# Moving half of one output projection earlier, adding its strips off TensorE, and running the other projection in half-width strips, in a two-attention decode kernel

## The chip, the cores and the metric

The kernel runs on one core of a Trainium2 chip. The time is the device time of one execution in microseconds (us). A second number, the *span*, runs from the first to the last instruction in the trace of the program. Times inside a trace are counted from the start of the span.

TensorE is the matmul engine, VectorE and ScalarE the two engines that read its results from PSUM. In profile lines they are PE (PEld for its weight loads), DVE and ACT; SPq is the queue that issues the DMAs.

## The reference

Two attention layers decode one token each; the two results are joined.

```python
# A: 32 heads, each with its own K and V of 32768 x 128
q = (x @ wq).reshape(B, Sq, H, Dh).transpose(0, 2, 1, 3)
p = softmax(einsum("bhqd,bhkd->bhqk", q, k_cache) * Dh ** -0.5)
o = einsum("bhqk,bhkd->bhqd", p, v_cache)
a = o.transpose(0, 2, 1, 3).reshape(B, Sq, H * Dh) @ wo      # (4096,) @ (4096, 512)
# B: the same with 8 shared K/V heads and the last 4096 keys only
out = concatenate([a, b], axis=-1)
```

All data is bf16. Some 570 MB have to be read, nearly all of it K and V of A.

## The kernel before

A short first stage does all of B's attention. A loop over A's 32 heads follows: transposes of K on TensorE, copies of these by VectorE, scores, softmax, and PV (probabilities times V). VectorE reduces PV's four strips into `oc`, and a *gather* matmul adds the head's row to a collecting PSUM bank. Last come the two output projections with `wo`, each as 32 matmuls of one output row ("row" a below) accumulated in PSUM. Wo is loaded at the end of the load queue, behind the last K and V.

```python
        for g in range(NQH):
            self.loop = {"pe": g, "dve": g // 2}
            self.load_k(g, 1 if 0 < g < NQH - 1 else 2)
            self.load_v(g)
            self.emit_qcopy(g)
            self.emit_unit("A", g)          # transposes of K and scores
            self.emit_stats("A", g)         # softmax
            self.emit_PT("A", g)
            self.emit_PV("A", g)            # PV, reduction by VectorE, gather
        self.loop = {}
        for n in ("B", "A"):
            for part in range(len(self.WO_CUTS[n]) - 1):
                self.load_wo(n, part)
        self.emit_spread("A")               # divide by the sums, turn o for the projection
        self.emit_proj()

    WO_CUTS = {"A": (0, 11, 19, 25, 29, 31, 32), "B": (0, 16, 32)}   # the parts in which Wo is loaded

    def halves(self, e, bank, lhsT, rhs, begin, end, only=(0, 1)):   # one row as two strips of 256
        for i in only:
            inst = e.matmul(bank[64 * i:64 * i + 1, 0:256], lhsT=lhsT, rhs=rhs[:, 256 * i:256 * i + 256], start=begin,
                            stop=end, tile_position=(0, 64 * i), skip_group_check=True)
        return inst

    def emit_proj(self):
        top = self.WO_CUTS["A"][1]
        for part in range(len(self.WO_CUTS["B"]) - 1):       # B: rows go to four strips, 32 partitions apart
            o = self.proj_part("B", part, lambda e, lhsT, rhs, a: e.matmul(
                self.S[32 * (a % 4):32 * (a % 4) + 1, :], ...))
        strips = self.op("dve", lambda v: v.tensor_copy(self.pb[:, :], self.S[:, :]), o)
        rows = o = self.op("pe", lambda e: e.matmul(self.ACC[0:1, :], lhsT=self.e32[:, 0:1], rhs=self.pb[:, :], ...))
        o = self.op("dve", lambda v: v.tensor_copy(self.qrow[0:1, :], self.ACC[0:1, :]), o)
        # ... B's half of the output leaves ...
        row = self.proj_part("A", 0, ...)                     # A, part 0: rows 0 to 10 at full width
        row = self.op("dve", lambda v: v.tensor_copy(self.pb[0:1, :], self.T[1][0:1, :]), row, rows)
        for part in range(1, len(self.WO_CUTS["A"]) - 1):     # A, the other parts: two half-width strips
            if part == 3:                                     # add the row of part 0
                self.op("pe", lambda e: self.halves(e, self.PT, self.e32[0:1, 0:1], self.pb[0:1, :], False, False), row)
            self.proj_part("A", part, ...)
        # ... row 31, stores of the two halves by VectorE and ScalarE, output DMA ...
```

## Time and profile before

| what | before |
|---|---|
| time, 3 runs | 1323.59 us (1322.69 to 1323.95) |
| span of the profiled run | 1321.7 us |
| bytes loaded, mean rate | 570.6 MB at 432 GB/s |
| last landing of a load (Wo of A, last part) | 1318.82 |
| start of the final stores | 1320.05 |

Three lines of the profile page of the kernel before: busy time of the engines (share of the span), the DMA's packets and rate, and the share of the 16 DMA engines' time that the load queue took.

```profile
PE 968.2 (73%) x13243; PEld 673.7 (51%) x13243; DVE 750.7 (57%) x1341; ACT 55.1 (4%) x168; POOL 2.6 (0%) x22
DMA packets 13359, 570.59 MB, mean 432 GB/s; under 512 B 1570, under 2 KB 1700, under 8 KB 2084
q1 hardware_dynamic: 13060, 570.43, 99.8%
```

The load queue is never out of work. The Trainium skill ("DMA: Bandwidth & Descriptors", Specifications) puts the fabric's ceiling at 435 GB/s, and the trace's 432 agrees. So the body of the kernel is a wall of bytes. What can still move is what comes after the last landing.

The chain of waits of the kernel before, its last 20 us. Columns: start, length, what ran (engine, output, line, count).

```profile
1300.21 6.30 PE psACC L656 x49
1306.52 0.08 PE psG L683 x2
...
1308.19 0.42 PE psG L683 x2
...
1309.67 3.27 PE psS L733 x32
...
1312.97 0.70 DVE pb L736
...
1313.71 1.02 PE psACC L737 x2
1314.73 2.27 PE psT L741 x11
1317.01 3.02 PE psPT L719 x42
...
1320.05 0.41 DVE out_sb L726
```

No load is in this chain: PV (L656), the gather (L683), B's projection (L733), the copy and row sum of B's strips (L736, L737), A's first part (L741) and its other parts (L719) follow one another on TensorE, and the last store starts at 1320.05, which is 1.23 us after the last landing.

The windows view of the kernel before near the end. Columns: stretch, its length, busy us of PE, PEld, DVE, ACT and POOL with instruction counts, the granted TensorE clock (1.00 is full), the DMA share, GB/s.

```profile
1309.00:1310.00 1.00, 0.60 (x12) 0.29 (x16) 0.35 (x2) 0.00 (x0) 0.00 (x0) 0.55 0.92 394
...
1311.00:1312.00 1.00, 1.00 (x16) 0.28 (x8) 0.00 (x0) 0.00 (x0) 0.00 (x0) 0.50 0.96 408
1312.00:1313.00 1.00, 0.91 (x12) 0.14 (x4) 0.03 (x1) 0.00 (x0) 0.00 (x0) 0.75 0.99 420
...
1318.00:1319.00 1.00, 1.00 (x13) 0.35 (x10) 0.00 (x0) 0.00 (x0) 0.00 (x0) 1.00 0.17 57
1319.00:1320.00 1.00, 1.00 (x16) 0.52 (x14) 0.00 (x0) 0.00 (x0) 0.00 (x0) 1.00 0.00 0
```

The DMA has stopped by 1319 while TensorE works for another microsecond. And B's projection ran at half clock: the third number from the end is 0.50.

### The profile page before, as it was taken

The numbers are of one execution on the slowest core, as the hardware profiler recorded it, in microseconds if no ns is written. First come the engines' busy times: TensorE is split into PE (matmuls) and PEld (weight loads), VectorE is DVE, ScalarE is ACT, GpSimd is POOL, SyncE is SP. The second block draws the span as 40 slices with busy tenths as digits, with TensorE's granted clock in tenths as the row PEclk, the third lists the DMA queues.
The fourth block names the chain that finished last, engine by engine and source line by source line (L and its number), as shares of the span: only waits on it lengthen the run. The fifth ranks groups of instructions, "written<-read, shape, count | busy, mean of one in ns | idle before, by whom it ended". The sixth has DMA issues, their size and how long they took to land. (4 is left out here: it accounts for less than half of the span.)

```text
span 1321.7 us, 28783 instructions
## 1 busy us (share of the span) xinstructions
PE 968.2 (73%) x13243; PEld 673.7 (51%) x13243; DVE 750.7 (57%) x1341; ACT 55.1 (4%) x168; POOL 2.6 (0%) x22
## 2 busy tenths in 40 slices
PE   4675768777677878767787777678777667877787
PEld 3353446555444655544465544446554445555453
DVE  3563556664555666455566645556665456665563
ACT  0000000000000000000000000000000000000000
POOL 0000000000000000000000000000000000000000
PEclk9886788887878888787888878888887788888788
DMA  9999999999999999999999999999999999999998
GB/s 404 434 434 431 440 434 434 434 436 432 433 436 436 428 438 434 428 438 434 428 442 430 428 442 432 430 438 434 437 432 432 438 430 434 438 428 436 436 428 365
DMA packets 13359, 570.59 MB, mean 432 GB/s; under 512 B 1570, under 2 KB 1700, under 8 KB 2084
## 3 DMA queue, kind: packets, MB, share of 16 engines
q1 hardware_dynamic: 13060, 570.43, 99.8%
q8 instruction: 8, 0.13, 0.0%
q10 hardware_dynamic: 288, 0.00, 0.0%
q14 instruction: 3, 0.02, 0.0%
HBM read 570.43 MB, written 0.00 MB: 432 GB/s over the span
## 5 line engine op out<-in xcount | busy, mean ns | idle before, releaser
L557 DVE COPY kt<-psT 128x1024 bf16<-128x1024 bf16 x1056 | 654.3, 683 | 236.9 <-PE psT L553 235.5
L553 PE MATMUL psT<-ident,kbuf 128*128 128x128 bf16 x8448 | 577.8, 234 | 169.0 <-DMA kbuf<-in_A_k_cache_dram 154.4
L553 PEld LDWEIGHTS psT<-ident,kbuf 128*128 128x128 bf16 x8448 | 538.1, 106 | 261.2 <-DMA kbuf<-in_A_k_cache_dram 162.5
L656 PE MATMUL psACC<-vbuf,ptsb 128*4 128x512 bf16 (+1 forms) x2112 | 187.0, 531 | 22.8 <-ACT ptsb L631 22.0
L576 PE MATMUL psS<-kt,qw 128*32 128x512 bf16 x2048 | 157.7, 385 | 14.9 <-DVE kt L557 14.9
L670 DVE TENSOR_SCALAR oc_A<-psACC,hot_A 128x128 f32<-128x128 f32 x32 | 11.2, 350 | 251.9 <-PE psG L683 251.9
L656 PEld LDWEIGHTS psACC<-vbuf,ptsb 128*4 128x4 bf16 (+1 forms) x2112 | 59.8, 111 | 140.4 <-issue 93.1
L604 ACT ACTIVATE psb<-psS,nb_A 128x512 bf16<-128x512 f32 x32 | 22.0, 687 | 1166.5 <-DVE nb_A L603 1166.5
L576 PEld LDWEIGHTS psS<-kt,qw 128*32 128x32 bf16 x2048 | 34.0, 95 | 57.6 <-DVE kt L557 30.8
L683 PE MATMUL psG<-oc_A,hw 128*32 128x128 f32 (+1 forms) x128 | 19.3, 227 | 52.3 <-DVE oc_A L672 52.3
L683 PEld LDWEIGHTS psG<-oc_A,hw 128*32 128x32 f32 x128 | 11.4, 109 | 62.4 <-DVE oc_A L672 55.0
L628 PE MATMUL psPT<-ident,psb 128*128 128x128 bf16 x136 | 18.3, 279 | 34.0 <-ACT psb L604 34.0
L672 DVE SCALAR_TENSOR_TENSOR oc_A<-psACC,hot_A,oc_A 128x128 f32<-128x128 f32 x96 | 33.6, 350 | 3.4
L593 DVE TENSOR_REDUCE tr_in<-psS 128x1 f32<-128x512 f32 x34 | 23.5, 692 | 17.2 <-PE psS L576 17.2
L628 PEld LDWEIGHTS psPT<-ident,psb 128*128 128x128 bf16 x136 | 10.3, 119 | 37.1 <-ACT psb L604 36.7
L597 PE MATMUL psACC<-rows,tr_in 128*1 128x64 f32 x64 | 8.7, 217 | 25.6 <-DVE tr_in L593 25.6
L631 ACT ACTIVATE ptsb<-psPT 128x512 bf16<-128x512 bf16 x34 | 20.3, 597 | 30.9 <-PE psPT L628 30.9
L597 PEld LDWEIGHTS psACC<-rows,tr_in 128*1 128x1 f32 x64 | 2.7, 81 | 35.1 <-DVE tr_in L593 35.1
L601 PE MATMUL psACC<-mr_A,nscale 1*128 1x1 f32 x64 | 12.1, 256 | 9.8 <-DVE mr_A L600 9.8
L601 PEld LDWEIGHTS psACC<-mr_A,nscale 1*128 1x128 f32 x64 | 9.4, 182 | 15.8 <-DVE mr_A L600 15.8
L603 DVE COPY nb_A<-psACC 128x1 f32<-128x1 f32 x32 | 5.0, 157 | 15.1 <-PE psACC L601 15.1
L600 DVE TENSOR_REDUCE mr_A<-psACC 1x1 f32<-1x64 f32 x32 | 6.8, 213 | 11.7 <-PE psACC L597 11.7
(82 smaller groups left out, 74.9 us busy)
## 6 DMA issues: line engine op xcount, KB each, us to landing
kbuf<-in_A_k_cache_dram SPq DMA_DIRECT2D x4, 4096.0 KB, 23.2
kbuf<-in_B_k_cache_dram SPq DMA_DIRECT2D x2, 4096.0 KB, 31.6
vbuf<-in_B_v_cache_dram SPq DMA_DIRECT2D x2, 4096.0 KB, 25.4
vbuf<-in_B_wq_dram SPq DMA_DIRECT2D x1, 4096.0 KB, 12.4
vbuf<-in_A_wq_dram SPq DMA_DIRECT2D x1, 4096.0 KB, 31.9
kbuf<-in_B_wo_dram SPq DMA_DIRECT2D x2, 2048.0 KB, 33.1
kbuf<-in_A_wo_dram SPq DMA_DIRECT2D x1, 1408.0 KB, 27.4
kbuf<-in_A_wo_dram SPq DMA_DIRECT2D x1, 1024.0 KB, 29.5
```

The source lines that it names most:

```text
L553: inst = e.transpose(T[:, 128 * k:128 * k + 128], src[:, DH * k:DH * k + DH], self.ident[:, :])
L557: self.copies.append(self.op("dve", lambda v: v.tensor_copy(KT[:, :], T[:, :]), o, to="pe"))
L576: inst = e.matmul(self.S[32 * c:32 * c + 32, :], lhsT=win, rhs=self.kt[(bb + c // 2) % NKT][:, 512 * (c % 2):512 * (c % 2) + 512], start=b ...
L593: o = dve(lambda v: v.reduce_max(tr["in"][:, 0:1], self.S[:, :], axis=AXX), self.sdone, self.k_pool, to="pe" if name == "A" else None)
L597: o = self.op("pe", lambda e: e.matmul(self.ACC[0:1, 0:64], lhsT=tr["in"][:, 0:1], rhs=self.rows64[:, :], start=True, stop=True, skip_grou ...
L601: o = self.op("pe", lambda e: e.matmul(self.ACC[:, 64:65], lhsT=self.nscale[:, :], rhs=t["mr"][0:1, :], start=True, stop=True, skip_group_ ...
L604: self.sread = self.op("act", lambda s: s.activation(out=self.psb[:, :], in_=self.S[:, :], func=ACTF.Exp, bias=t["nb"][:, k:k + 1], scale= ...
L628: inst = e.transpose(PT[:, 128 * jj:128 * jj + 128], self.psb[:, 128 * jj:128 * jj + 128], self.ident[:, :])
L631: self.ptread = self.op("act", lambda s: s.activation(out=self.ptsb[:, :], in_=PT[:, 0:512], func=ACTF.Copy), self.psread, to="pe")
L656: inst = e.matmul(acc[32 * c:32 * c + rows, 0:512], lhsT=lhsT, rhs=rhs, start=begin, stop=end, tile_position=(0, 32 * c), skip_group_check ...
L672: o = self.op("dve", lambda v, src=src, hot=hot: v.scalar_tensor_tensor(out=oc, in0=src, scalar=hot, in1=oc, op0=ALU.mult, op1=ALU.add), p ...
L683: return self.op("pe", lambda e: e.matmul(self.G[0:32, c0 + c:c0 + c2], lhsT=win, rhs=t["oc"][g % len(t["oc"])][:, c:c2], start=False, sto ...
```

## The change

The intent is to shorten TensorE's last stretch in four ways:

1. The gather of head g moves from the end of pass g to the top of pass g + 1, so the last one can be placed freely behind the loop.
2. Half of B's projection runs before that last gather, in TensorE's wait for VectorE.
3. B's four strips are added by VectorE and ScalarE instead of by a copy and an fp32 matmul.
4. All of A's rows run as two half-width strips, so there is no full-width row to be added to them.

```diff
             self.emit_qcopy(g)
+            self.gath = self.emit_gather("A", g - 1, 0, DH)
             self.emit_unit("A", g)
@@
+        self.emit_proj_b(0)
+        self.gath = self.emit_gather("A", NQH - 1, 0, DH)
         self.emit_spread("A")
         self.emit_proj()
@@
         self.accread = o
-        self.gath = self.emit_gather(name, g, 0, DH)
+        if name == "B":
+            self.gath = self.emit_gather(name, g, 0, DH)
@@ (cut: the new helper emit_proj_b, one part of B's projection as before)
+    def sum_strips(self, o):
+        S = [self.S[32 * c:32 * c + 1, :] for c in range(STRIPS)]
+        row = [self.kt[c][0:1, :].bitcast(F32) for c in range(STRIPS)]
@@ (cut: helpers)
+        two = self.op("dve", lambda v: v.tensor_copy(row[2], S[2]), o, to="act")
+        one, three = act(1), act(3)
+        x = add(row[0], S[0], row[1], o, one)
+        y = add(row[2], row[2], row[3], two, three)
+        return add(self.qrow[0:1, :], row[0], row[2], x, y)
@@
-        strips = self.op("dve", lambda v: v.tensor_copy(self.pb[:, :], self.S[:, :]), o)
-        rows = o = self.op("pe", lambda e: e.matmul(self.ACC[0:1, :], lhsT=self.e32[:, 0:1], ...
-        o = self.op("dve", lambda v: v.tensor_copy(self.qrow[0:1, :], self.ACC[0:1, :]), o)
+        o = self.emit_proj_b(1)
+        o = self.sum_strips(o)
@@
-        row = self.proj_part("A", 0, ...)
-        row = self.op("dve", lambda v: v.tensor_copy(self.pb[0:1, :], self.T[1][0:1, :]), row, rows)
-        for part in range(1, len(self.WO_CUTS["A"]) - 1):
-            if part == 3:
-                self.op("pe", lambda e: self.halves(e, self.PT, self.e32[0:1, 0:1], self.pb[0:1, :], False, False), row)
-            self.proj_part("A", part, lambda e, lhsT, rhs, a: self.halves(e, self.PT, lhsT, rhs, a == top, False)
+        for part in range(len(self.WO_CUTS["A"]) - 1):
+            self.proj_part("A", part, lambda e, lhsT, rhs, a: self.halves(e, self.PT, lhsT, rhs, a == 0, False)
                            if a < 31 else None)
```

The first gather of the loop has no head before it; `oc` and its selection `hw` are set to zero for it, which is cut here.

More of the change, by code (lines that the diff above doesn't have):

```diff
@@ L284, in alloc @@
         self.m4 = sb("m4", [1, 128], F32)
-        self.pb = sb("pb", [128, 512], F32)
         self.out_sb = sb("out_sb", [1, 512], BF16)
@@ L456, in constants @@
             pattern=[[-32, 4], [-1, 16]], compare_op=ALU.is_equal, fill=0.0, base=0, channel_multiplier=1), rows)
+        pool(lambda g: g.memset(c["A"]["oc"][0][:, :], 0.0))
+        self.k_hw = pool(lambda g: g.memset(self.hw[:, :], 0.0))
         pool(lambda g: g.memset(self.nscale[:, :], -self.SCALE))
@@ L460, in constants @@
             self.k_pool = pool(lambda g, n=n: g.memset(c[n]["b"][:, :], 0.0))
-        self.k_hw = pool(lambda g: g.memset(self.hw[:, :], 0.0))
         dve = lambda fn, *deps, **k: self.op("dve", fn, *deps, **k)
@@ L684, in emit_gather @@
             self.G[0:32, c0 + c:c0 + c2], lhsT=win, rhs=t["oc"][g % len(t["oc"])][:, c:c2], start=False, stop=True,
-            skip_group_check=True), self.accread, self.sread, self.hcopy if name == "A" else self.k_sel, to="dve")
+            skip_group_check=True), *(self.accread, self.sread, self.hcopy if name == "A" else self.k_sel) if g >= 0 else
+            (self.k_hw, self.accread), to="dve")
     def emit_spread(self, name):
@@ L727, in store @@
         return self.op("act", lambda e: e.activation(out=out, in_=src, func=ACTF.Copy), dep)
-    def emit_proj(self):
-        top = self.WO_CUTS["A"][1]
-        for part in range(len(self.WO_CUTS["B"]) - 1):
-            o = self.proj_part("B", part, lambda e, lhsT, rhs, a: e.matmul(
-                self.S[32 * (a % 4):32 * (a % 4) + 1, :], lhsT=lhsT, rhs=rhs, start=(a < 4), stop=(a >= 28),
-                tile_position=(0, 32 * (a % 4)), skip_group_check=True))
-        strips = self.op("dve", lambda v: v.tensor_copy(self.pb[:, :], self.S[:, :]), o)
-        rows = o = self.op("pe", lambda e: e.matmul(self.ACC[0:1, :], lhsT=self.e32[:, 0:1], rhs=self.pb[:, :], start=True,
-                                             stop=True, skip_group_check=True), strips, self.accread)
-        o = self.op("dve", lambda v: v.tensor_copy(self.qrow[0:1, :], self.ACC[0:1, :]), o)
-        self.op("sp", lambda e: e.dma_start(self.out[0, :, 512:1024], self.qrow[0:1, :]).then_inc(self.outsem["B"], 16), o)
-        row = self.proj_part("A", 0, lambda e, lhsT, rhs, a: e.matmul(
-            self.T[1][0:1, :], lhsT=lhsT, rhs=rhs, start=(a == 0), stop=(a == top - 1), skip_group_check=True))
-        row = self.op("dve", lambda v: v.tensor_copy(self.pb[0:1, :], self.T[1][0:1, :]), row, rows)
-        for part in range(1, len(self.WO_CUTS["A"]) - 1):
-            if part == 3:
-                self.op("pe", lambda e: self.halves(e, self.PT, self.e32[0:1, 0:1], self.pb[0:1, :], False, False), row)
-            self.proj_part("A", part, lambda e, lhsT, rhs, a: self.halves(e, self.PT, lhsT, rhs, a == top, False)
@@ new lines, in emit_proj_b @@
+    def emit_proj_b(self, part):
+        return self.proj_part("B", part, lambda e, lhsT, rhs, a: e.matmul(
+            self.S[32 * (a % 4):32 * (a % 4) + 1, :], lhsT=lhsT, rhs=rhs, start=(a < 4), stop=(a >= 28),
+            tile_position=(0, 32 * (a % 4)), skip_group_check=True))
+    def sum_strips(self, o):
+        S = [self.S[32 * c:32 * c + 1, :] for c in range(STRIPS)]
+        row = [self.kt[c][0:1, :].bitcast(F32) for c in range(STRIPS)]
+        dve = lambda fn, *deps: self.op("dve", fn, *deps)
+        act = lambda c: self.op("act", lambda e: e.activation(out=row[c], in_=S[c], func=ACTF.Copy), two)
+        add = lambda out, a, b, *deps: dve(lambda v: v.tensor_tensor(out=out, in0=a, in1=b, op=ALU.add), *deps)
+        two = self.op("dve", lambda v: v.tensor_copy(row[2], S[2]), o, to="act")
[3 more added lines that the diff above has]
+        return add(self.qrow[0:1, :], row[0], row[2], x, y)
```

## The prediction

> **What bounds the kernel.** The page's DMA line: 570.6 MB at a mean of 432 GB/s, the load queue taking 99.8% of 16 engines' span. The Trainium skill ("DMA: Bandwidth & Descriptors", Specifications) gives a fabric ceiling of 435 GB/s; this trace agrees, so all but the last microseconds is a wall of bytes that the change does not touch. TensorE (73% busy) and VectorE (57%) have slack. Only what comes after the last landings can move.
>
> **The tail.** From the DMA issue times plus times to landing (us from the span's start): V of the last head lands at 1299.2; Wo of B in two parts at 1304.2 and 1308.9; the six parts of A's Wo at 1312.2, 1314.8, 1316.7, 1317.9, 1318.4 and 1318.9. In the windows view the DMA share falls to half at 1317 and to zero at about 1318.4. The chain of waits ends: B's projection 3.27 us, VectorE copy 0.70, fp32 row sum 1.02, A's first part at full width 2.27, the rest in halves 3.02 with the fp32 addition of the row in it (0.52), stores from 1320.05, output DMA issued 1320.55, end 1321.7. So TensorE ends about 1.1 us after the last weights landed: that backlog is the prize.
>
> **What the change does.**
> - Half of B's projection (16 of 32 matmuls, about 1.65 us) moves into the 1.64 us in which TensorE waits for VectorE's last reduction (idle before the final gather). Its weights landed at 1304.2, so nothing waits.
> - The copy and fp32 row sum leave TensorE's way: 0.76 + 1.02 us. In their place VectorE and ScalarE do six one-row operations of 0.4 to 0.7 us, hidden under A's projection.
> - A's first 11 rows cost 0.133 us a pair of halves (14 halves took 0.93 us) instead of 0.206 at full width: 0.8 us less; the row's copy and fp32 addition go (0.52 us).
> - The gather of the previous head goes to the top of the next pass. VectorE's reduction then overlaps the loop's branch: about 1 us of TensorE per pass. In the loop it buys nothing, the DMA bounds; in the last pass PV can start just when V lands, up to 0.9 us earlier.
>
> TensorE work of some 4 to 5 us leaves the tail, but A's parts then wait for their weights. Estimate: B's second half from 1308.9 to 1310.6; A's parts each 1.46, 1.06, 0.80, 0.53 and 0.27 us after their landings, so each ends before or about when the next lands. The last pair starts at 1318.95, 0.27 us to the first half, stores from about 1319.25 instead of 1320.05. Gain 0.8 us of 1323.6, or 0.06%, inside the run-to-run spread of 1.3.
>
> **Prediction:** 1322.8 us, 8 in 10 between 1321.9 and 1323.7. Faster by over 2%: 0.003; within 2%: 0.994; slower: 0.003.
>
> **What the profile would show.** Right: mean GB/s and the loop's groups unchanged; B's first half directly before the final gather; TensorE idle before several of A's parts, released by the DMA of A's weights; stores starting within 0.4 us of the last landing. The clock (granted 0.5 from about 1309.5 to 1312.5 now) may fall elsewhere. By the Trainium skill ("TensorE: Matmul & The Clock Gate", Part 1) idle windows halve it; a cold final stretch would double the last parts' matmul time and eat 0.2 to 0.5 us.
>
> **What would make it wrong.** The last landing moving by itself; a cold clock for A's parts; the early half of B's projection delaying the gather.

## The result, and the profile after

| | before | after |
|---|---|---|
| time, 6 runs each | 1322.76 us (1322.49 to 1323.95) | 1322.66 us (1321.93 to 1323.56) |
| ratio, 95% interval | | 0.9998 (0.9985 to 1.0011) |
| span of the profiled run | 1321.7 us | 1320.6 us |
| last landing | 1318.82 | 1318.63 |
| start of the final stores | 1320.05 | 1318.98 |
| stores behind the last landing | 1.23 us | 0.35 us |

A ratio here is the mean time of one kernel's fast runs over that of the other's of the same rounds, so it is not quite the ratio of the medians quoted. The kernel before is at 1323.59 us in the first table and at 1322.76 here because three more runs have been added.

The same three lines of the page of the kernel after:

```profile
PE 966.4 (73%) x13250; PEld 676.3 (51%) x13250; DVE 752.3 (57%) x1342; ACT 56.3 (4%) x170; POOL 2.8 (0%) x23
DMA packets 13359, 570.59 MB, mean 432 GB/s; under 512 B 1570, under 2 KB 1700, under 8 KB 2084
q1 hardware_dynamic: 13060, 570.43, 99.9%
```

The wall is as it was. The chain of waits of the kernel after, its last 37 us:

```profile
1283.20 28.90 DMA kbuf<-in_A_wo_dram
1312.10 0.04 issue
1312.15 4.31 PE psPT L724 x38
1316.46 0.03 issue
1316.49 2.46 PE psPT L724 x25
...
1318.98 0.41 DVE out_sb L731
```

Now a load stands at the head of the chain: A's projection (L724) starts when the first part of Wo lands and goes on as the others land. The timeline of the kernel after shows what became of TensorE's time (columns: start, length, engine, line, operation, shapes, count; in brackets the idle time before it and what ended it):

```profile
1299.16 5.92 PE L659 MATMUL psACC<-vbuf,ptsb 128*4 128x512 bf16 x64 [1.26 <-DMA vbuf<-in_A_v_cache_dram]
...
1304.97 1.02 PE L736 MATMUL psS<-kbuf,oz_B 128*1 128x512 bf16 x13
...
1306.75 0.41 PE L687 MATMUL psG<-oc_A,hw 128*32 128x128 f32 x2 [0.75 <-DVE oc_A L675]
...
1308.82 1.03 PE L736 MATMUL psS<-kbuf,oz_B 128*1 128x512 bf16 x16 [0.78 <-DMA kbuf<-in_B_wo_dram]
...
1312.15 6.80 PE L724 MATMUL psPT<-kbuf,oz_A 128*1 128x256 bf16 x64 [2.29 <-DMA kbuf<-in_A_wo_dram]
```

PV starts with V's landing (1299.02). B's first half (L736, 1304.97) sits before the last gather (L687). TensorE waits for loads three times: 1.26 us for V, 0.78 us for B's second part and 2.29 us for A's first. What left TensorE came back as waits.

The windows view of the kernel after:

```profile
1316.00:1317.00 1.00, 0.97 (x12) 0.35 (x8) 0.00 (x0) 0.00 (x0) 0.00 (x0) 0.50 1.01 398
1317.00:1318.00 1.00, 1.00 (x16) 0.49 (x14) 0.00 (x0) 0.00 (x0) 0.00 (x0) 0.75 0.62 235
1318.00:1319.00 1.00, 0.95 (x14) 0.21 (x8) 0.02 (x1) 0.00 (x0) 0.00 (x0) 1.00 0.11 36
```

The half-clock stretch has moved into A's projection, and it cost nothing that shows, since that projection waits for its weights and the last rows ran at full clock again.

One trace of each says: 1.07 us gained at the stores (1320.05 to 1318.98). Six runs of each say: 0.1 us in the median, far inside the interval. The experiments ask what the profiled gain is made of, and why the repeated runs show less of it.

### The profile page after: what moved, and what is told of

Read it like the earlier page. It is cut to its first block, busy times and chain, and to the rows that moved or that the text cites. A ratio compares the mean times of both kernels' runs of the same rounds, so it can differ in the third digit from the quotient of the medians.

```text
span 1320.6 us, 28803 instructions
## 1 busy us (share of the span) xinstructions
PE 966.4 (73%) x13250; PEld 676.3 (51%) x13250; DVE 752.3 (57%) x1342; ACT 56.3 (4%) x170; POOL 2.8 (0%) x23
## 2 busy tenths in 40 slices
DMA packets 13359, 570.59 MB, mean 432 GB/s; under 512 B 1570, under 2 KB 1700, under 8 KB 2084
## 4 chain that ended last, share of the span: by engine, by line
DMA 70%; PE 28%; DVE 1%; issue 0%; ACT 0%; SPq 0%
DMA kbuf<-in_A_k_cache_dram 65%; PE psT L556 24%; PE psS L579 4%; DMA kbuf<-in_B_k_cache_dram 3%; DMA kbuf<-in_A_wo_dram 2%; DVE kt L560 1%; PE psPT L724 1%; PE psACC L659 0%; DVE oc_A L675 0%; ACT psb L607 0%; PE psPT L631 0%; DVE tr_in L596 0%; ACT ptsb L634 0%; PE psG L687 0%; DVE out_sb L731 0%
## 5 line engine op out<-in xcount | busy, mean ns | idle before, releaser
L659 PE MATMUL psACC<-vbuf,ptsb 128*4 128x512 bf16 (+1 forms) x2112 | 182.3, 520 | 23.3 <-ACT ptsb L634 21.3
L687 PE MATMUL psG<-oc_A,hw 128*32 128x128 f32 (+1 forms) x130 | 19.9, 229 | 52.1 <-DVE oc_A L675 51.5
L687 PEld LDWEIGHTS psG<-oc_A,hw 128*32 128x32 f32 x130 | 11.6, 109 | 62.7 <-DVE oc_A L675 54.6
```

Of the source, the lines that this page charges most:

```text
L659: inst = e.matmul(acc[32 * c:32 * c + rows, 0:512], lhsT=lhsT, rhs=rhs, start=begin, stop=end, tile_position=(0, 32 * c), skip_group_check ...
L687: return self.op("pe", lambda e: e.matmul(self.G[0:32, c0 + c:c0 + c2], lhsT=win, rhs=t["oc"][g % len(t["oc"])][:, c:c2], start=False, sto ...
```

## The experiments

The theory at the start: the kernel before ends with a backlog of TensorE behind the last landing; the landing plus about 0.35 us is a floor; any one part of the change that removes more than the backlog reaches the floor, and the rest turns into waits. Rival 1: the four parts add up, each with its share. Rival 2: the load stream itself ends earlier. Later a third question came up: why the kernel before is sometimes at the floor already.

Spans are compared below, because they are steadier than times: before, the time is 1.6 to 1.8 us above the span in all of 25 runs; after, it is 1.3 to 2.9 us above in 10 runs. What fills that difference is in no trace, and it moves with the edits: it was 1.40 to 1.47 us in the four runs of sum_only below and 1.57 to 3.11 us in those of halves_only. So a gain in the span is not yet one in the time. Each list of spans has the profiled run first, then the repeats.

### The two kernels again

No edit. The kernel before:

> The kernel before, unchanged, for its spread. Both theories: span 1321.3 to 1322.0 us; in the profile the stores start 1.1 to 1.3 us after the last part of A's Wo has landed (1.23 in the first trace), with TensorE waiting for no load after the last head's PV.

Measured: spans 1321.9, 1321.6, 1321.5, 1320.8; time 1322.52 to 1323.58. Last landing 1318.84, stores 1320.28, so 1.44 us behind it, more than the 1.1 to 1.3 expected; and the lowest span was below the expected band. The chain of waits of this second run of the kernel before:

```profile
1276.73 2.76 PE psT L553 x24
...
1302.24 5.94 PE psACC L656 x61
...
1311.31 1.86 PE psS L733 x32
...
1317.23 3.02 PE psPT L719 x42
...
1320.28 0.41 DVE out_sb L726
```

The same end, but another path to it: PV started 2.03 us later than in the first trace (1302.24 against 1300.21), while B's projection took 1.86 us instead of 3.27. The backlog is not one number of the kernel.

> The changed kernel, unchanged, for its spread. Span 1320.5 to 1321.1 us; stores 0.35 us after the last landing.

Measured: spans 1320.7, 1320.8, 1320.8, 1320.7; last landing 1318.78, stores 1319.13, 0.35 us behind it, as expected.

### One part at a time

Three kernels, each the kernel before with one part of the change.

```diff
# gather_only: before, and
+            self.gath = self.emit_gather("A", g - 1, 0, DH)     # top of the pass, and once behind the loop
-        self.gath = self.emit_gather(name, g, 0, DH)             # end of the pass, for A
# sum_only: before, and
-        strips = ... ; rows = o = ... ; o = ...                  # copy, fp32 row sum, cast
+        o = self.sum_strips(o)
# halves_only: before, and
-        row = self.proj_part("A", 0, ...) ...                    # part 0 at full width, copy, addition
+        for part in range(len(self.WO_CUTS["A"]) - 1): ...       # all parts in halves
```

> Only the gather moved to the top of the next pass. Theory (the prize is TensorE's backlog behind the last landing, so any one part of the change that removes about 0.9 us of TensorE's last stretch wins all of it): PV of the last head starts within 0.2 us of V's landing instead of 1.0 us after it, the chain of 19.84 us from there ends at the last landing plus 0.35 to 0.5 us, span about 0.8 to 0.9 us shorter than before's. Rival 1 (the four parts each add their share of the 1.1 us): 0.2 to 0.4 us shorter, stores 0.8 to 1.0 us after the last landing. Rival 2 (the gain is that the load stream ends earlier because the loop frees buffers earlier): stores still 1.2 us after the last landing, and the last landing itself about 1 us earlier.

> Only B's strips added by VectorE and ScalarE instead of a copy and an fp32 row sum on TensorE. Theory: 1.78 us leave TensorE's last stretch, more than the backlog, so stores start 0.35 to 0.45 us after the last landing and the span is 0.8 to 0.9 us shorter than before's; the rest becomes waits for A's weights. Rival 1: 0.3 to 0.4 us shorter. Rival 2: no gain, as the loop is that of before.

> Only A's first part in halves, and so no row to be added. Theory: 0.8 + 0.52 us leave TensorE, more than the backlog, stores 0.35 to 0.5 us after the last landing, span 0.7 to 0.9 us shorter. Rival 1: 0.2 to 0.4 us shorter. Rival 2: no gain.

| kernel | spans | mean span | time, median | last landing | stores behind it |
|---|---|---|---|---|---|
| before, same chip, 7 runs | 1320.7 to 1321.6 | 1321.20 | 1322.92 | | |
| gather_only | 1321.0, 1321.5, 1321.5, 1321.0 | 1321.25 | 1322.95 | 1319.00 | 0.36 us |
| sum_only | 1320.8, 1320.8, 1321.0, 1321.2 | 1320.95 | 1322.33 | 1318.86 | 0.35 us |
| halves_only | 1320.8, 1320.7, 1320.7, 1321.1 | 1320.83 | 1322.95 | 1318.79 | 0.35 us |

In each of the three traces the stores start 0.35 to 0.36 us behind the last landing: with every single part the end is at the floor that all four together reach. That speaks against rival 1, which expected 0.8 to 1.0 us for gather_only.

By itself this is weak evidence, for the unchanged kernel reaches the floor too in two of four traces (see the last experiment). What matters is how fast B's projection ran. The timeline of gather_only:

```profile
1308.50 3.27 PE L738 MATMUL psS<-kbuf,oz_B 128*1 128x512 bf16 x32
```

And of sum_only:

```profile
1308.52 1.90 PE L746 MATMUL psS<-kbuf,oz_B 128*1 128x512 bf16 x32
...
1312.38 2.54 PE L751 MATMUL psT<-kbuf,oz_A 128*1 128x512 bf16 x11 [1.97 <-DMA kbuf<-in_A_wo_dram]
```

In gather_only the projection was as slow as in the first trace of before, and the end was at the floor all the same, because PV started 0.14 us after V's landing instead of 1.00 us; this compares like with like. In sum_only and halves_only it ran at full clock, 1.90 us. Their traces show the parts' effect only in the waits: TensorE waited for parts of Wo for 1.97 and 0.86 us in sum_only, and for 0.53, 0.82 and 0.41 us in halves_only. A slow projection would have added about 1.4 us (3.31 less 1.90), which these waits would have taken up; that is an estimate.

Rival 2 falls too: its last landing about 1 us earlier is not there; in gather_only it is 0.2 us later than in the first trace of before.

But the sizes were missed. Expected were spans 0.7 to 0.9 us shorter than before's; measured are 0.05 us longer, 0.25 and 0.37 us shorter on the mean. The profiled gather_only run reached the floor with nothing to spare (TensorE waited no more than 0.04 us for the parts of A's Wo), and two of its repeats, with spans of 1321.5 us, were longer by 0.5 us. Over its four runs the mean gained nothing.

### Three parts without the early half of B

```diff
-        self.emit_proj_b(0)                       # before the last gather
         self.gath = self.emit_gather("A", NQH - 1, 0, DH)
@@ emit_proj
+        self.emit_proj_b(0)
         o = self.emit_proj_b(1)
```

> The changed kernel with B's first half back behind the spread of A's result, next to its second half. Theory: the other parts remove more than the backlog, so the last landing still ends the chain: stores 0.35 us after it, span as the changed kernel's within 0.2 us. Rival 1 (parts add): 0.2 to 0.5 us longer than the changed kernel's.

Measured: spans 1320.8, 1321.4, 1320.7, 1320.8, mean 1320.92 beside 1320.75 of the changed kernel on the same chip; last landing 1318.86, stores 1319.21, 0.35 us behind. The profile is as the theory expects. The mean is within 0.2 us, but one run of four (1321.4) lies outside, so a small share of the early half in the worst runs is not excluded.

### Less to load

To lower the floor, 2.1 MB of the load stream (the second part of B's Wo) are left out, in both kernels. The first part is used twice, so the result of B is wrong.

```diff
-                self.load_wo(n, part)
+                if (n, part) != ("B", 1):
+                    self.load_wo(n, part)
@@ proj_part
+        cut = 16 if (name, part) == ("B", 1) else 0
-                inst = out(e, oz[:, a:a + 1], wo[:, 512 * a:512 * a + 512], a) or inst
+                inst = out(e, oz[:, a:a + 1], wo[:, 512 * (a - cut):512 * (a - cut) + 512], a) or inst
-        deps = (self.wosem[name][part], 16), self.c[name]["ozop"]
+        deps = (self.wosem[name][0 if name == "B" else part], 16), self.c[name]["ozop"]
```

> The kernel before with the second half of B's Wo not loaded (2.1 MB less; the first half is used twice, so the result of B is wrong on purpose). Theory: all landings of A's Wo come 4.8 us earlier (2.1 MB at 432 GB/s), but TensorE's chain from V's landing on does not wait for them: stores stay at about 1320.0, span 1321.4 to 1321.7, at most 0.3 us shorter than before's. Rival 2 (the stream's end sets the end of the kernel before too): span about 4 to 4.8 us shorter.

> The changed kernel with the same 2.1 MB not loaded (result of B wrong on purpose). Theory: here the landings bound, so it gains from them until TensorE's work bounds again: stores at 1314.2 (TensorE at full clock) to 1316.3 (half clock), span 1315.7 to 1317.9, so 4 to 6 us shorter than the kernel before with the same bytes: the size of what the change took from TensorE's last stretch. Rival 1 (the change took only about 1 us from TensorE): about 1 us shorter than the kernel before with the same bytes.

| kernel | spans | mean span | last landing | stores |
|---|---|---|---|---|
| before, same chip, 7 runs | 1320.5 to 1322.0 | 1321.17 | | |
| before_less | 1319.5, 1321.6, 1319.2, 1321.1 | 1320.35 | 1313.90 | 1317.92 |
| after_less | 1315.9, 1315.8, 1316.0, 1316.1 | 1315.95 | 1313.98 | 1314.34 |

The chain of waits of before_less, its end:

```profile
1308.95 1.86 PE psS L735 x32
...
1314.87 3.02 PE psPT L721 x42
...
1317.92 0.41 DVE out_sb L728
```

And of after_less:

```profile
1285.88 27.17 DMA kbuf<-in_A_wo_dram
...
1313.74 0.58 PE psPT L726 x5
...
1314.34 0.41 DVE out_sb L733
```

The landings came 4.9 us earlier than in the first trace of before. The kernel before gained 0.82 us of that on the mean, and its stores are 4 us behind the landing; rival 2 is out. The changed kernel gained 5.2 us against before on the same chip, and still ends 0.36 us behind the last landing. So with the same bytes the change is worth 4.4 us on the mean (1320.35 to 1315.95); between the stores of the two profiled runs it is 3.58 us. The changed kernel's TensorE work was still not the bound, so what left TensorE's last stretch is that much or more. With all bytes loaded the wall hides it.

Two details missed: the profiled stores of before_less are at 1317.92 and not at about 1320.0, and its spans differ by 2.4 us among themselves, with nothing of the load stream in the chain's last part. TensorE's chain has a spread of its own. The kernel before shows only what sticks out above the floor.

### Filler matmuls

In both traces of before, stretches of TensorE's chain ran at half clock, and not the same ones. So the next idea was to keep the clock up with 17 small matmuls a pass, in TensorE's waits between the last scores and PV.

```diff
+    def fill_pe(self, n):                          # n matmuls of the identity into a free PSUM bank
@@ A only
+        self.fill_pe(6)                            # after the last scores
+        self.fill_pe(6)                            # before the transposes of the probabilities
+        self.fill_pe(5)                            # before PV
```

> The kernel before with 2.1 MB of B's Wo not loaded (as in before_less, whose spans were 1319.2 to 1321.6 us) and with 17 filler matmuls of 128 columns a pass, placed in TensorE's waits for VectorE and ScalarE between the last scores and PV (result of B wrong on purpose, as there). Theory: the kernel before ends with TensorE's chain, and that chain's length changes from run to run with where the half-clock windows fall; fillers keep the clock at full over PV, which then takes 3.5 to 5 us instead of 5.8 to 6.3: span 1316.5 to 1318.5, spread under 1.2 us. Rival (the spread comes from when the last loads land or from anything but the clock): spans 1319 to 1321.6 as without fillers. If the granted clock over PV is still 0.5, the test tells nothing.

> The kernel before with the same fillers and all loads (correct result). Theory: as TensorE's chain gets at least 1 us shorter, the last landing bounds: stores 0.35 to 0.5 us after it, spans 1320.6 to 1321.1 as in the changed kernel, though nothing of the projections was changed. Rival: spans 1320.5 to 1322.0 as in the kernel before, stores 0.8 us or more after the last landing.

Measured: warm_less 1319.1, 1320.4, 1318.6, 1318.8 (mean 1319.22, without fillers 1320.35, on another chip); warm 1320.7, 1320.7, 1321.7, 1321.6 (mean 1321.17; before on the same chip 1321.04). The windows view of warm_less:

```profile
1298.00:1300.00 2.00, 1.59 (x14) 1.06 (x11) 0.00 (x0) 1.30 (x4) 0.00 (x0) 0.50 0.90 385
...
1308.00:1310.00 2.00, 2.00 (x24) 0.46 (x16) 0.00 (x0) 0.00 (x0) 0.00 (x0) 0.50 0.99 415
```

The test fell short. The fillers moved the half-clock stretches (the mean clock rose only from 0.838 to 0.862), and one of them lay over B's projection again. PV took 4.13 us (58 of its 64 matmuls in the chain), inside the expected 3.5 to 5, but the spans are above the expected 1316.5 to 1318.5. In the profiled run of warm the clock was at half over the first transposes of the last pass (5.02 us) and at 1.00 from 1298 to the end; PV took 3.63 us there, and the stores were 0.35 us behind the landing. Two of its repeats were at 1321.6 and 1321.7. Fillers of this size don't hold the clock in every run.

### The kernel before, twice more

If the theory is right that the end of the kernel before is the later of a fixed floor and a moving chain, then unchanged copies of it must show both cases.

> The kernel before once more, for a third trace of its end. Theory: its end is the later of two things, the last landing plus 0.35 us and TensorE's chain, whose length moves with the half-clock windows. So a span of at most 1320.9 us goes with stores within 0.5 us of the last landing and a load of Wo in the chain that ended last; a span above 1321.2 us goes with stores 0.8 us or more after it and no load in the chain, and the last landing lies at 1318.6 to 1319.0 us in either. Rival: the span's spread comes from the load stream, so a shorter span goes with an earlier last landing and the stores stay 1.2 us behind it.

> The same, a fourth trace of the kernel before: as for the third.

Measured: spans 1320.8 and 1320.6, so both fell into the short case. The chain of waits of the third trace:

```profile
1275.91 3.82 PE psT L553 x64
...
1285.83 30.84 DMA kbuf<-in_A_wo_dram
1316.67 0.04 issue
1316.71 2.46 PE psPT L719 x29
...
1319.20 0.41 DVE out_sb L726
```

A load is in the chain, the last landing is at 1318.85, and the stores are 0.35 us behind it. The fourth: 1318.67, stores at 1319.02, again 0.35 us. The kernel before, unchanged, is at the floor in these two runs. The four traces of it differ mainly in two places (durations from the timeline, which counts a matmul's whole time, so B's projection is 0.04 us longer than in the chain). PV differs less: 6.30, 5.95, 5.84 and 5.83 us, and in all four most of it ran at half clock.

| trace of before | 64 first transposes of the last pass | PV starts | B's projection | last landing | stores behind it | span |
|---|---|---|---|---|---|---|
| first | 3.82 us | 1300.21 | 3.31 us | 1318.82 | 1.23 us | 1321.7 |
| again | 5.13 us | 1302.24 | 1.90 us | 1318.84 | 1.44 us | 1321.9 |
| third | 3.82 us | 1300.36 | 1.90 us | 1318.85 | 0.35 us | 1320.8 |
| fourth | 3.82 us | 1300.08 | 1.90 us | 1318.67 | 0.35 us | 1320.6 |

The granted clock goes with it. The windows view over those transposes, in the second trace and then in the third:

```profile
1276.00:1280.00 4.00, 3.27 (x34) 3.28 (x35) 1.87 (x3) 0.00 (x0) 0.00 (x0) 0.57 1.10 475
```

```profile
1276.00:1280.00 4.00, 4.00 (x72) 3.61 (x72) 3.43 (x6) 0.00 (x0) 0.00 (x0) 1.00 1.10 475
```

At 0.57 TensorE put 34 matmuls through in 3.27 busy us; at 1.00 it was 72 in 4.00. The Trainium skill ("TensorE: Matmul & The Clock Gate", Part 1) says that the clock is at half or at full and is decided in free-running windows of 3413 ns, which do not start anew with the kernel. The traces agree: in the first one the half-clock stretch over B's projection lasts from 1309.1 to 1312.5, 3.4 us, and the one over PV from 1298.9 to 1305.7, about twice that. In one run such a window falls on B's projection, in another on the last pass's first transposes, in a third on neither. In the two runs where it falls on either, the chain outlasts the landing by over 1 us.

The durations account for the ends. With 1.90 us for B's projection instead of 3.31, the first trace's chain would have ended 1.41 us earlier, at about 1318.6 and so before its floor (1318.82 plus 0.35); that is an estimate. In the second trace the slow transposes are not the whole cause: its last pass began 0.96 us later than the first's (1276.73 against 1275.77), since half-clock stretches had lain longer over the pass before (first transposes 5.76 against 5.15 us, PV 6.29 against 5.95). Without these 0.96 us its backlog would have been about 0.5 us instead of 1.44; that too is an estimate.

So the rival of this last test falls: the two short runs have the same last landing as the long ones, within 0.2 us. That the clock's windows decide which case a run falls in rests on these durations in four traces, which all fit; it was not forced, as the test meant to do that (the fillers) was too weak. For the repeats there are spans alone.

## Why the prediction was right or wrong

- **"A wall of bytes that the change does not touch"**: right. 432 GB/s and 570.59 MB before and after; the last landing lies between 1318.63 and 1319.00 in every trace with all bytes.
- **B's first half in the wait for VectorE, before the final gather**: right. It took about 1.07 us (1304.92 to 1305.99), not 1.65, as it ran at full clock; 0.75 us of the wait were left.
- **The copy and row sum, and the full-width part, leave TensorE's way**: right, and their total was about right. Predicted were "some 4 to 5 us"; with the wall lowered, the change was worth 4.4 us on the mean and 3.58 us between the profiled runs, and still ended at the floor.
- **"A's parts then wait for their weights"**: right. 2.29 us before the first part, then part by part; stores expected about 1319.25 and seen at 1318.98, with a last landing 0.2 to 0.3 us earlier than reckoned. "Within 0.4 us of the last landing" was 0.35.
- **PV starts when V lands**: right, 0.14 us after it.
- **The clock may fall elsewhere**: right. Half clock from about 1310.7 to 1317.5, over most of A's projection, without cost.
- **"That backlog is the prize", 0.8 us of gain**: this term was mis-sized. It was read from one trace, as if it belonged to the kernel. It belongs to the run: 1.23, 1.44, 0.35 and 0.35 us from landing to stores in four traces of the same kernel, of which 0.35 is the floor. Over 25 runs of the kernel before the spans are 1320.5 to 1322.0, mean 1321.19; over 10 runs of the changed one 1320.6 to 1321.1, mean 1320.79 (several chips; on the one chip with both in one comparison, 1321.17 and 1320.75). The gain is 0.4 us on the mean span, half of what was said, and the changed kernel's spread is a third of the other's (standard deviations 0.14 and 0.43 us). In time it does not show: the means of the same runs are 1322.89 and 1322.62, with standard deviations of 0.42 and 0.60. That the predicted 1322.8 came so near to the measured 1322.66 is in part luck: it is a gain of 0.8 taken off 1323.6, the median of three runs of the kernel before, whose median over six runs is 1322.76. Both errors, the start and the gain, were about as large and cancel.

Where the expected gain went: of the 4 to 5 us that TensorE lost, all but the part that stuck out behind the last landing became waits for loads.

## What to carry to other kernels

Behind a saturated load stream only the backlog after the last landing can be won, whatever is cut from TensorE's work, and in the traces here any one cut about as large as the backlog was enough (though gather_only's, of about 0.9 us, was not in two of its four runs): look at whether the chain of waits ends in a load before adding a second cut. To see what a cut would be worth without the wall, leave out some bytes on purpose and compare both kernels there. And before pricing a backlog of a microsecond from one trace, take several traces of the unchanged kernel, since half-clock windows of some 3.4 us fell differently in each here.

## What the Trainium skill lacked or had wrong

- "TensorE: Matmul & The Clock Gate", Part 4, says that the full clock does not engage for transposes on TensorE. Here 64 transposes (a K tile against the identity, the kernel's transpose calls) took 3.82 us, 60 ns each. The windows view of the kernel before, in a stretch where four of five TensorE instructions are such transposes, has the granted clock at 1.00 (below). In the second trace the clock even rose from 0.50 to 1.00 while nothing but 64 transposes ran (1241.27 to 1247.0), after 5.12 us of waiting for K. Whether the page means a mode that these calls do not set is not shown; their lines in the trace say MATMUL.

```profile
1281.00:1285.00 4.00, 4.00 (x68) 2.94 (x66) 4.00 (x8) 0.00 (x0) 0.00 (x0) 1.00 0.94 410
```

- The same clock page, in Part 1, says that the number of slow matmuls at a kernel's start changes from run to run with the free-running window. It has no figure for the end of a long kernel: here an unchanged one ended up to 1.3 us apart (spans of 1320.6 to 1321.9 in four traces), and that went with where the windows fell.
- "Runtime: NRT & Kernel Launch" lists what runs before and after a kernel, but not which of it the device time counts beyond the traced span. Here that was 1.6 to 1.8 us in 25 runs of the kernel before, 1.3 to 2.9 us in 10 runs of the changed one.
